# Issuing a rearrangement and its DMA transpose one to seven steps earlier, in an attention + MoE kernel

## The chip, the cores and the metric

The kernel runs on one core of a Trainium2 chip. The metric is the device time of one execution in microseconds (us), lower is better. The matmuls take bf16 and accumulate in fp32. Each run also has a granted TensorE clock and a state: on one core a run counts as slow when it is over 1.5% above the fastest run of the same kernel.

## The reference, cut to what matters

For each of 8 batches and 8 heads, x is (512, 64) and state is (32, 64). There are two reads with softmax, then a feed-forward layer over all 4352 rows.

```python
scores = scale * x @ state.T ; a = softmax(scores)        # (512, 32)
xread  = a @ state
sread  = softmax(scale * state @ x.T) @ x                 # (32, 64)
rows   = concat([xread, sread])  ->  (B * 544, 512)       # heads side by side
out    = gelu(rows @ w_in) @ w_out                        # 512 -> 2048 -> 512
```

## The kernel before

The kernel is a software pipeline with a hand-made schedule. While TensorE runs the feed-forward matmuls of batch b (16 steps; in each, `mm1` of batch b and `mm2` of batch b - 1), a table inserts the attention work of the next batch into some of the steps. The scores of a batch need x transposed. The path of the data is: a load of x by GpSimd (POOL) into `xb`, a rearrangement into `x4`, and a DMA transpose from `x4` into `xT`, issued by SyncE (SP), which also issues the output writes.

```python
xin = tile_pool(bufs=3)                  # xb: three batches
att = tile_pool(bufs=2)                  # xT, e, a, ...: two batches
x4s = [tile x4_0, tile x4_1]             # two batches, fixed
...
def load_x(b):      nc.gpsimd.dma_start(out=xb, in_=x[b]...)       # 512 KB as bf16, cast from fp32 on the way
...
load_x(1); load_w_in(2); load_w_in(3); load_w_out(0); load_w_out(1)
load_x(2); load_w_out(2); load_w_out(3); load_x(3)                 # at start-up
...
def rearr(b):       eng = nc.vector if b < 3 else nc.gpsimd
                    # two copies: xb -> x4
def xtr_dma(b):     nc.sync.dma_start_transpose(out=A.xT..., in_=A.x4...)
def atr_dma(b):     nc.sync.dma_start_transpose(out=A.AT..., in_=A.a)   # later, of the softmax
def scores(b, half): # TensorE: pt <- xT, sbd (L189); ScalarE: exp (L199)
def sread(b):       # TensorE: sr <- e, x4 (L269)
...
extra = {
    ...
    1: {
        1: [sread(0), pmat(1, (2,))],
        2: [srt(0)],
        3: [pmat(1, (3,)), begin(2), rearr(2), xtr_dma(2)],
        4: [load_x(4), sread(1)],
        6: [srt(1)],
        8: [scores(2, 0), scores(2, 1), norm(2, 0), norm(2, 1)],
        10: [pmat(2, (0, 1), ...)],  11: [atr_dma(2)],  13: [sread(2)],
        14: [pmat(2, (2, 3), ...)],  15: [srt(2)],
    },
}
def steady(b):      # b >= 2
    nb = b + 1
    d[0] = [begin(nb), rearr(nb)];  if b + 3 < B: d[0].append(load_x(b + 3))
    d[0].append(xtr_dma(nb))
    d[4] = [scores(nb, 0), scores(nb, 1), norm(nb, 0), norm(nb, 1)]
    d[7] = [pmat(nb, (0, 1), ...)];  d[8] = [atr_dma(nb)];  d[12] = [sread(nb)]
    d[13] = [pmat(nb, (2, 3), ...)];  d[14] = [srt(nb)]
```

(The `lambda:` around every entry of the tables is left out here and below.)

The softmax here doesn't subtract the row's maximum and nothing guards it: scores larger than these inputs give would overflow.

Of the kernel before, what the change touches and what calls it, by code (L numbers as in the profile page):

```python
# [17 lines left out]
def kernel(  # L18
# [10 lines left out]
    B, H, S, D = x.shape  # L29
# [63 lines left out]
    def load_x(b):  # L93
        xb = xin.tile([128, H, SJ * D], BF16, name="xb", tag="xb")
        nc.gpsimd.dma_start(out=xb, in_=x[b].rearrange("h (p j) d -> p h (j d)", j=SJ))
        xbs[b] = xb
# [48 lines left out]
    def begin(b):  # L145
        A = Att()
        atts[b] = A
        A.x4 = x4s[b % 2]
        A.xT = att.tile([128, SJ, HC, 128], BF16, name="xT", tag="xT")
        A.e = att.tile([128, SJ * 2, HC * NS], BF16, name="e", tag="e")  # L150
        A.a = att.tile([128, SJ * 2, HC * NS], BF16, name="a", tag="a")

    def rearr(b):
        A = atts[b]
        eng = nc.vector if b < 3 else nc.gpsimd
        for t in range(2):
            eng.tensor_copy(  # L157
                out=A.x4[:, :, :, 64 * t:64 + 64 * t].rearrange("p j c d -> p c j d"),
                in_=xbs[b][:, 4 * t:4 * t + 4, :].rearrange("p c (j d) -> p c j d", d=D),
            )  # L160
# [45 lines left out]
    def xtr_dma(b):  # L206
        A = atts[b]
        nc.sync.dma_start_transpose(
            out=A.xT.rearrange("p j c n -> p (j c) n"), in_=A.x4.rearrange("p j c n -> p (j c n)")
        )  # L210

    def scores(b, half):
        score_mms(b, 2 * half)
        score_mms(b, 2 * half + 1)
        expo(b, half)

    def norm(b, half):
        A = atts[b]
        G = SJ * 2
        hs = slice(64 * half, 64 * half + 64)  # L220
        e4 = A.e[:, :, hs].rearrange("p g (c n) -> p g c n", n=NS)
        cs = att.tile([128, G, 2], FP32, name="cs", tag="cs")
        nc.vector.reduce_sum(out=cs, in_=e4, axis=AX.X)  # L223
        ics = att.tile([128, G, 2], FP32, name="ics", tag="ics")
        nc.vector.reciprocal(out=ics, in_=cs)
        nc.vector.tensor_tensor(  # L226
            out=A.a[:, :, hs].rearrange("p g (c n) -> p g c n", n=NS),
            in0=e4,
            in1=ics[:, :, :].to_broadcast((128, G, 2, NS)),
            op=ALU.mult,  # L230
        )
# [21 lines left out]
    def atr_dma(b):  # L253
        A = atts[b]
        A.AT = att.tile([128, SJ, 2, 128], BF16, name="AT", tag="AT")
        nc.sync.dma_start_transpose(
            out=A.AT.rearrange("p j t n -> p (j t) n"), in_=A.a
        )


    def sread(b):
        A = atts[b]
        sr = ps_f.tile([128, 130], FP32, name="sr", tag="f")
        for o, n in ((0, D), (128, 1)):
            for t in range(2):
                for j in range(SJ):
                    for c in range(HC):
                        q = slice(32 * c, 32 * c + 32)
                        nc.tensor.matmul(  # L269
                            sr[q, o + n * t:o + n * t + n],  # L270
                            lhsT=A.e[:, 2 * j + t, q],
                            rhs=A.x4[:, j, c, 64 * t:64 * t + 64] if n == D else ones,
                            start=(j == 0),
                            stop=(j == SJ - 1),
                        )
        A.srm = att.tile([128, 2, D], BF16, name="srm", tag="srm")
        inv = att.tile([128, 2], FP32, name="inv", tag="inv")
        nc.vector.reciprocal(out=inv, in_=sr[:, 128:130])
        nc.vector.tensor_tensor(
            out=A.srm,  # L280
            in0=sr[:, 0:128].rearrange("q (t d) -> q t d", t=2),
            in1=inv[:, :].to_broadcast((128, 2, D)),
            op=ALU.mult,
        )

    def srt(b):
        A = atts[b]
        ps = ps_f.tile([128, HC, NS], BF16, name="srT", tag="f")
        nc.tensor.transpose(
            ps.rearrange("p c n -> p (c n)"), A.srm.rearrange("q t d -> q (t d)"), ident  # L290
        )
        nc.vector.tensor_copy(out=XSR[:, :, b * NS:(b + 1) * NS], in_=ps)
# [3 lines left out]
    def pmat(b, fs, act=()):  # L296
        if b not in Ps:
            Ps[b] = att.tile([128, 2, d_ff], BF16, name="P", tag="P")
        pss = []
        for f in fs:  # L300
            ps = [ps_f.tile([128, 512], FP32, name="p_ps", tag="f") for t in range(2)]
            for c in range(HC):
                for t in range(2):
                    nc.tensor.matmul(  # L304
                        ps[t][32 * c:32 * c + 32, :],
                        lhsT=sbd[64 * t:64 * t + 64, b, c, 32 * t:32 * t + 32],
                        rhs=w_in_bf[64 * t:64 * t + 64, c, f * 512:(f + 1) * 512],
                        start=True,
                        stop=True,
                    )  # L310
            pss.append(ps)
        for f, ps in zip(fs, pss):
            for t in range(2):
                dst = Ps[b][:, t, f * 512:(f + 1) * 512]
                if (f, t) in act:
                    nc.scalar.copy(out=dst, in_=ps[t])  # L316
                else:
                    nc.vector.tensor_copy(out=dst, in_=ps[t])  # L318
# [86 lines left out]
    for c in range(HC):  # L405
# [32 lines left out]
        },  # L438
        1: {
            1: [lambda: sread(0), lambda: pmat(1, (2,))],  # L440
            2: [lambda: srt(0)],
            3: [lambda: pmat(1, (3,)), lambda: begin(2), lambda: rearr(2), lambda: xtr_dma(2)],
            4: [lambda: load_x(4), lambda: sread(1)],
            6: [lambda: srt(1)],
            8: [lambda: scores(2, 0), lambda: scores(2, 1), lambda: norm(2, 0), lambda: norm(2, 1)],
# [1 line left out]
            11: [lambda: atr_dma(2)],  # L447
            13: [lambda: sread(2)],
            14: [lambda: pmat(2, (2, 3), act=((2, 1), (3, 1)))],
            15: [lambda: srt(2)],  # L450
        },
    }

    def steady(b):
        nb = b + 1
        d = {}
        if nb >= B:
            return d
        d[0] = [lambda: begin(nb), lambda: rearr(nb)]
        if b + 3 < B:  # L460
            d[0].append(lambda: load_x(b + 3))
        d[0].append(lambda: xtr_dma(nb))
        d[4] = [
            lambda: scores(nb, 0),
            lambda: scores(nb, 1),
            lambda: norm(nb, 0),
            lambda: norm(nb, 1),
        ]
        d[7] = [lambda: pmat(nb, (0, 1), act=((0, 1), (1, 1)))]
        d[8] = [lambda: atr_dma(nb)]  # L470
        d[12] = [lambda: sread(nb)]
        d[13] = [lambda: pmat(nb, (2, 3), act=((2, 1), (3, 1)))]
        d[14] = [lambda: srt(nb)]
        return d
# [4 lines left out]
    for b in range(B):  # L479
        plan = extra[b] if b in extra else steady(b)  # L480
        for s in range(MC):
            for f in plan.get(s, ()):
                f()
            mm1(b, s)
            done += 1
            if done > lag:
                mm2(u)
                u += 1
# [40 lines left out]
```

## Time and profile before

| before | |
|---|---|
| time, median of 3 runs | 236.54 us (236.05 to 237.08) |
| span of the profiled run, granted clock | 234.7 us, 0.999 |
| TensorE busy | 217.1 us |
| TensorE waiting for xT | 5.4 us in six waits |

The prediction below shows the page, the waits and one steady batch. Two more readings matter later. The first is TensorE's timeline at the scores of batches 2, 3 and 5, where the bracket gives the idle time before the row and what ended it:

```profile
44.76 0.64 PE L189 MATMUL pt<-sbd,xT 128*128 128x64 bf16 x16 [0.88 <-DMA xT<-x]
...
65.92 0.64 PE L189 MATMUL pt<-sbd,xT 128*128 128x64 bf16 x16 [1.78 <-DMA xT<-x]
...
115.33 0.64 PE L189 MATMUL pt<-sbd,xT 128*128 128x64 bf16 x16 [1.44 <-DMA xT<-x]
```

The second is POOL's timeline around the end of start-up: the loads of batch 3 and, because POOL runs far ahead of the schedule, of batch 4, then nothing until the rearrangement of batch 3, which waits for its load.

```profile
21.27 0.89 POOL L95 DMA_DIRECT2D xb<-in_x_dram  x1 [0.57 <-DMA w_in_bf<-in_moe_w_in_dram]
22.92 0.88 POOL L95 DMA_DIRECT2D xb<-in_x_dram  x1 [0.76 <-DMA w_in_bf<-in_moe_w_in_dram]
40.20 2.02 POOL L157 COPY x<-xb 128x1024 bf16<-128x1024 bf16 x2 [16.40 <-DMA xb<-in_x_dram]
42.16 0.88 POOL L95 DMA_DIRECT2D xb<-in_x_dram  x1
```

These rows are only the issues. The view of the DMA issues gives the landings: 18.8 us after issue for batch 3 (at 40.1) and 19.8 us for batch 4 (at 42.7; the prediction's 42.2 came from a median of the two). The x load with least in its way, issued at 80 us, takes 5.9 us. The transpose of batch 2 is issued as SP's timeline shows:

```profile
38.62 4.07 SPq L208 DMA_TRANSPOSE xT<-x  x1
```

### The profile page before, as it was taken

The numbers are of one execution on the slowest core, as the hardware profiler recorded it, in microseconds if no ns is written. First come the engines' busy times: TensorE is split into PE (matmuls) and PEld (weight loads), VectorE is DVE, ScalarE is ACT, GpSimd is POOL, SyncE is SP. The second block draws the span as 40 slices with busy tenths as digits, with TensorE's granted clock in tenths as the row PEclk, the third lists the DMA queues.
The fourth block names the chain that finished last, engine by engine and source line by source line (L and its number), as shares of the span: only waits on it lengthen the run. The fifth ranks groups of instructions, "written<-read, shape, count | busy, mean of one in ns | idle before, by whom it ended". The sixth has DMA issues, their size and how long they took to land.

```text
span 234.7 us, 4315 instructions
## 1 busy us (share of the span) xinstructions
PE 217.1 (92%) x1844; PEld 100.7 (43%) x1844; DVE 85.3 (36%) x162; ACT 124.7 (53%) x208; POOL 28.1 (12%) x38
## 2 busy tenths in 40 slices
PE   5996799889979999999799999999999999999993
PEld 1543244434334444444344444444444444567441
DVE  2655974274135413631181317231623111111120
ACT  2577754485467446744494549454955454426000
POOL 8745001304000400030002000000000000000000
PEclk9999999999999999999999999999999999999999
DMA  7999999972923294252804061316131111211122
GB/s 205 149 178 206 202 205 185 126 161 26 226 76 86 56 165 98 62 75 53 128 0 106 31 143 38 89 47 134 46 92 45 47 45 55 80 46 47 27 65 87
DMA packets 38707, 23.12 MB, mean 98 GB/s; under 512 B 21920, under 2 KB 34464, under 8 KB 38688
## 3 DMA queue, kind: packets, MB, share of 16 engines
q0 software_dynamic: 13376, 8.09, 25.3%
q1 hardware_dynamic: 24352, 14.03, 24.8%
q10 hardware_dynamic: 960, 0.72, 1.0%
q8 instruction: 14, 0.23, 0.4%
q14 instruction: 5, 0.04, 0.1%
HBM read 17.30 MB, written 8.91 MB: 112 GB/s over the span
## 4 chain that ended last, share of the span: by engine, by line
PE 68%; DMA 18%; DVE 5%; ACT 3%; POOL 3%; issue 1%; SPq 1%; POOLq 0%; ACTq 0%
PE op L362 37%; PE hp L328 18%; DMA xT<-x 13%; DMA xb<-in_x_dram 5%; PE hps L376 3%; PE ops L388 3%; PE p_ps L304 3%; PE sr L269 2%; PE pt L189 2%; ACT g L335 2%; DVE osb L348 1%; POOL w_in_bf L79 1%; DVE P L318 1%; DVE a L226 1%; DVE cs L223 1%
## 5 line engine op out<-in xcount | busy, mean ns | idle before, releaser
L362 PE MATMUL op<-w_out_bf,g 128*128 128x512 bf16 x512 | 130.2, 379 | 0.0
L335 ACT ACTIVATE g<-hp 128x512 bf16<-128x512 f32 x128 | 74.5, 602 | 61.9 <-PE hp L328 61.7
L328 PE MATMUL hp<-AT,P 128*128 128x512 bf16 x256 | 75.9, 380 | 2.9 <-DVE P L318 1.5
L362 PEld LDWEIGHTS <-g 128*128 128x128 bf16 x512 | 50.1, 98 | 58.7
L348 DVE COPY osb<-op 128x512 f32<-128x512 f32 x31 | 21.4, 690 | 88.8 <-PE op L362 88.8
L328 PEld LDWEIGHTS <-P 128*128 128x128 bf16 x256 | 22.5, 98 | 30.2 <-issue 6.6
L318 DVE CAST P<-p_ps 128x512 bf16<-128x512 f32 x38 | 24.3, 684 | 11.1 <-PE p_ps L304 11.1
L157 POOL COPY x<-xb 128x1024 bf16<-128x1024 bf16 x10 | 10.1, 1044 | 93.3 <-PE sr L269 76.9
L316 ACT CAST P<-p_ps 128x512 bf16<-128x512 f32 x26 | 14.1, 601 | 6.1 <-PE p_ps L304 6.1
L223 DVE TENSOR_REDUCE cs<-e 128x16 f32<-128x512 bf16 x16 | 10.9, 682 | 17.2 <-ACT e L199 17.2
L199 ACT ACT_TABLE_LOAD x7 | 9.0, 1283 | 9.7 <-PE pt L189 9.7
L189 PE MATMUL pt<-sbd,xT 128*128 128x64 bf16 x128 | 6.3, 200 | 6.2 <-DMA xT<-x 5.4
L304 PE MATMUL p_ps<-w_in_bf,sbd 64*32 64x512 bf16 x256 | 11.9, 384 | 0.1
L226 DVE TENSOR_TENSOR a<-e,ics 128x512 bf16<-128x512 bf16 x16 | 11.1, 692 | 0.6
L383 ACT ACTIVATE g_sr<-hps 128x256 bf16<-128x256 f32 x16 | 6.1, 384 | 8.4 <-PE hps L376 8.0
L335 ACT ACT_TABLE_LOAD x8 | 10.3, 1283 | 0.1
L189 PEld LDWEIGHTS <-xT 128*128 128x128 bf16 x128 | 4.9, 102 | 10.5 <-DMA xT<-x 8.4
L199 ACT ACTIVATE e<-pt 128x512 bf16<-128x512 f32 x16 | 8.8, 595 | 0.7 <-PE pt L189 0.6
L118 PE MATMUL warm_ps<-warm 128*128 128x512 bf16 x20 | 7.9, 542 | 1.2 <-DVE warm L73 1.2
L376 PE MATMUL hps<-XSR,w_in_bf 128*128 128x256 bf16 x64 | 8.5, 273 | 0.0
L345 ACT COPY osb<-op 128x256 f32<-128x256 f32 x1 | 0.4, 372 | 13.9 <-DVE osb L343 13.9
L376 PEld LDWEIGHTS <-w_in_bf 128*128 128x128 bf16 x64 | 6.3, 98 | 2.7
(48 smaller groups left out, 81.8 us busy)
## 6 DMA issues: line engine op xcount, KB each, us to landing
out_dram<-osb SPq DMA_DIRECT2D x31, 256.0 KB, 2.3
xb<-in_x_dram POOLq DMA_DIRECT2D x7, 512.0 KB, 11.6
w_in_bf<-in_moe_w_in_dram POOLq DMA_DIRECT2D x8, 256.0 KB, 10.1
w_out_bf<-in_moe_w_out_dram POOLq DMA_DIRECT2D x4, 512.0 KB, 14.9
x0f<-in_x_dram SPq DMA_DIRECT2D x2, 256.0 KB, 3.4
x0f<-in_x_dram ACTq DMA_DIRECT2D x2, 256.0 KB, 4.3
out_dram<-osb SPq DMA_DIRECT2D x8, 64.0 KB, 1.7
st_bf<-in_state_dram POOLq DMA_DIRECT2D x1, 224.0 KB, 10.2
```

What stands on the lines that cost most here:

```text
L189: nc.tensor.matmul(A.pt[:, j, :, c % 2, :], lhsT=A.xT[:, j, c, :], rhs=sbd[:, b, c, :], start=True, stop=True,)
L199: nc.scalar.activation(out=A.e[:, :, 64 * half:64 * half + 64], in_=A.pt.rearrange("p j t c n -> p (j t) (c n)"), func=AF.Exp, scale=scale,)
L223: nc.vector.reduce_sum(out=cs, in_=e4, axis=AX.X)
L226: nc.vector.tensor_tensor(out=A.a[:, :, hs].rearrange("p g (c n) -> p g c n", n=NS), in0=e4, in1=ics[:, :, :].to_broadcast((128, G, 2, NS) ...
L304: nc.tensor.matmul(ps[t][32 * c:32 * c + 32, :], lhsT=sbd[64 * t:64 * t + 64, b, c, 32 * t:32 * t + 32], rhs=w_in_bf[64 * t:64 * t + 64, c ...
L316: nc.scalar.copy(out=dst, in_=ps[t])
L318: nc.vector.tensor_copy(out=dst, in_=ps[t])
L328: nc.tensor.matmul(hp, lhsT=Ps[b][:, t, m * 128:(m + 1) * 128], rhs=atts[b].AT[:, :, t, :], start=(t == 0), stop=(t == 1),)
L335: nc.scalar.activation(out=gs[b][:, m, :], in_=hp, func=AF.Gelu)
L348: nc.vector.tensor_copy(out=osb, in_=ps)
L362: nc.tensor.matmul(ps, lhsT=gs[b][:, m, j * 128:(j + 1) * 128], rhs=w_out_bf[:, m, :], start=(m == 0), stop=(m == MC - 1),)
L376: nc.tensor.matmul(hp, lhsT=w_in_bf[:, c, m * 128:(m + 1) * 128], rhs=XSR[:, c, :], start=(c == 0), stop=(c == HC - 1),)
```

## The change

The intent is to take the wait for xT away from TensorE by issuing the transpose eleven steps before the scores in steady batches, in place of four.

```diff
 1: {
-    2: [srt(0)],
-    3: [pmat(1, (3,)), begin(2), rearr(2), xtr_dma(2)],
+    2: [srt(0), begin(2), rearr(2), xtr_dma(2)],
+    3: [pmat(1, (3,))],
...
-    15: [srt(2)],
+    15: [srt(2), begin(3), rearr(3), load_x(5), xtr_dma(3)],
 def steady(b):
-    d[0] = [begin(nb), rearr(nb)]
-    if b + 3 < B: d[0].append(load_x(b + 3))
-    d[0].append(xtr_dma(nb))
...
     d[8] = [atr_dma(nb)]
+    if nb + 1 < B:
+        d[9] = [begin(nb + 1), rearr(nb + 1)]
+        if nb + 3 < B: d[9].append(load_x(nb + 3))
+        d[9].append(xtr_dma(nb + 1))
```

So the change has three parts: batch 2 moves one step earlier, batch 3 moves one step earlier (from step 0 of batch 2 to step 15 of batch 1), and batches 4 to 7 move seven steps earlier.

More of the change, by code (lines that the diff above doesn't have):

```diff
@@ L440 @@
             1: [lambda: sread(0), lambda: pmat(1, (2,))],
-            2: [lambda: srt(0)],
-            3: [lambda: pmat(1, (3,)), lambda: begin(2), lambda: rearr(2), lambda: xtr_dma(2)],
+            2: [lambda: srt(0), lambda: begin(2), lambda: rearr(2), lambda: xtr_dma(2)],
+            3: [lambda: pmat(1, (3,))],
             4: [lambda: load_x(4), lambda: sread(1)],
@@ L449 @@
             14: [lambda: pmat(2, (2, 3), act=((2, 1), (3, 1)))],
-            15: [lambda: srt(2)],
+            15: [lambda: srt(2), lambda: begin(3), lambda: rearr(3), lambda: load_x(5), lambda: xtr_dma(3)],
         },
@@ L458, in steady @@
             return d
-        d[0] = [lambda: begin(nb), lambda: rearr(nb)]
-        if b + 3 < B:
-            d[0].append(lambda: load_x(b + 3))
-        d[0].append(lambda: xtr_dma(nb))
         d[4] = [
@@ L470, in steady @@
         d[8] = [lambda: atr_dma(nb)]
+        if nb + 1 < B:
+            d[9] = [lambda: begin(nb + 1), lambda: rearr(nb + 1)]
+            if nb + 3 < B:
+                d[9].append(lambda: load_x(nb + 3))
+            d[9].append(lambda: xtr_dma(nb + 1))
         d[12] = [lambda: sread(nb)]
```

## The prediction

> **What bounds the kernel now.** I read the page first: busy shares, then the chain that ended last, then the waits, then the timeline of one batch, then the DMA issues.
>
> ```profile
> PE 217.1 (92%) x1844; PEld 100.7 (43%) x1844; DVE 85.3 (36%) x162; ACT 124.7 (53%) x208; POOL 28.1 (12%) x38
> ...
> PE 68%; DMA 18%; DVE 5%; ACT 3%; POOL 3%; issue 1%; SPq 1%; POOLq 0%; ACTq 0%
> PE op L362 37%; PE hp L328 18%; DMA xT<-x 13%; DMA xb<-in_x_dram 5%; PE hps L376 3%; PE ops L388 3%; PE p_ps L304 3%; PE sr L269 2%; PE pt L189 2%; ACT g L335 2%; DVE osb L348 1%; POOL w_in_bf L79 1%; DVE P L318 1%; DVE a L226 1%; DVE cs L223 1%
> ```
>
> TensorE is busy for 217.1 of 234.7 us, so it bounds the kernel, with 17.6 us of idle to win at most. The chain puts 13% (30 us) on the transpose that makes xT from x. That figure is not what the transpose costs: while it is in flight TensorE goes on with the feed-forward matmuls (L328, L362), and the chain merely follows the DMA in place of that work. The cost is what TensorE waits at its end, which the list of waits gives:
>
> ```profile
> PEld L189 <- DMA xT<-x: 8.4, 6, 2.3
> ...
> PE pt L189 <- DMA xT<-x: 5.4, 6, 1.8
> ...
> PE hp L328 <- DVE P L318: 1.5, 4, 0.8
> ```
>
> The columns are the total in us, how often, and the longest. The score matmuls (L189) of batches 2 to 7 each wait once for xT: 5.4 us on TensorE's matmul row in six waits. The 8.4 us of weight loads is the same event seen from an engine that runs ahead, so it isn't added. After start-up the one other matmul wait is 1.03 us on ACT, in batch 1. The timeline of one steady batch shows why the DMA is late:
>
> ```profile
> 133.94 0.69 DVE L348 COPY osb<-op 128x512 f32<-128x512 f32 x1 [2.37 <-PE op L362]
> ...
> 134.66 0.33 SPq L350 DMA_DIRECT2D out_dram<-osb  x1
> ...
> 135.09 2.17 SPq L208 DMA_TRANSPOSE xT<-x  x1
> ...
> 138.06 1.03 PE L362 MATMUL op<-w_out_bf,g 128*128 128x512 bf16 x4
> ...
> 139.54 0.64 PE L189 MATMUL pt<-sbd,xT 128*128 128x64 bf16 x16 [0.45 <-DMA xT<-x]
> ```
>
> The transpose isn't held by its data: in the POOL timeline the rearrangement of this batch ended near 105. It is held by its place in SyncE's in-order stream, behind the output write of step 15, which waits for an eviction of VectorE at 133.94. Issued at 135.09, it lands 4.40 us later, 0.05 us before the scores start. Step 4 of the batch simply comes round too soon.
>
> **What the Trainium skill says.** "DMA: Bandwidth & Descriptors", Rules for kernel authors: issue a DMA early, compute, and wait on its semaphore late. That is the change, and the trace agrees that only the tail is exposed. "Perfetto Trace Analysis", Summary: the profiler window per engine type: the slice of a hardware-generated DMA leaves out the data movement, and a matmul's end is estimated. The trace agrees with the first (a 2.17 us slice, 4.40 us to landing). For the second, "TensorE: Matmul & The Clock Gate", Wait — 56ns, not 53.3ns?, gives 215.7 ns start to start for 512 columns; here the four matmuls from 138.06 would release the next at 138.92 (the hp pairs after other groups of four do start 0.86 us on), while the row shows an end at 139.09. So each wait is some 0.16 us longer than its idle column. "DMA: Bandwidth & Descriptors", Silent corruption: two transposing streams in flight at once: transposes from SP form one stream, so putting xT right behind AT needs no new wait. No trace here tests that, as the two are now 12 us apart.
>
> **The change part by part.** Nothing is added or removed: same instructions, bytes and shapes. What moves is where the transpose stands on SP and where the rearrangement stands on DVE (batch 2) or POOL (3 to 7).
>
> *POOL*: order there stays rearr 3, load 5, rearr 4, load 6, rearr 5, load 7, rearr 6, rearr 7. POOL already runs ahead: it does these at 40.2, 53.9, 78.2, 102.4 and 127.6, each released by a weighted-sum matmul (sr, L269) or, the first, by a load. All precede the new issue points (batch 4 at about 75, then 99, 124, 149). No gain, no loss.
>
> *Batches 4 to 7*: xT is issued behind the AT transpose of step 8 (for the batch shown, SP is done with AT at 147.50 + 1.30 = 148.8; the next scores run at 163.70). About 15 us of lead against 4.4 to 6.1 us to landing. The wait goes. By the idle column: 0.45, 1.44, 0.45, 0.44; with 0.16 each: 0.61, 1.60, 0.61, 0.60, sum **3.4 us**.
>
> *Batch 2*: one step earlier. Before: issued at 38.62, landed at 44.70 (6.08 us, beside the loads), score matmul at 44.76 instead of 42.85 + 0.86 = 43.71. After: its xb landed at 16.04 + 15.2 = 31.2, VectorE ends XSR at 35.13 and then idles 1.44 us for p_ps; the two copies (0.75 us) fit into that hole. Issue at about 36.0, landing near 42 to 43, even if the two loads in flight (until 40.1 and 42.2) slow it. Needed at 43.7. Gain **1.0 us**.
>
> *Batch 3*: step 15 in place of step 0. Before: issued at 60.14 behind the second of two output writes, landed at 65.87, needed at 63.12 + 0.86 = 63.98, a delay of 1.94 us. After: only the write of 58.37 stands ahead, so issue at about 58.7, 1.4 us earlier; at 5.7 us it lands at 64.4, leaving 0.4 to 0.6 us. A load that POOL issues at 55.91 and that takes 6.0 us now overlaps more of it. Gain **1.4 us**.
>
> Sum: 3.4 + 1.0 + 1.4 = **5.8 us**; all six waits gone altogether would be 6.4. 236.54 − 5.8 = **230.7 us**, 2.5% less.
>
> **The rivals.**
> 1. *A new wait takes its place.* After the scores, ACT does a table load (1.28), two exps (1.09) and another table load (1.28) while gelus queue up, and TensorE can run out of PSUM buffers; it does for 1.03 us in batch 1. But this burst starts when the scores end, so it moves with them. Before them, ACT idles 1.16 us in the batch shown; with the scores 0.6 us earlier some idle is left. If ACT or VectorE gave half of it back, time would be 233 to 234. I give it little.
> 2. *The transpose was hidden anyway*, as its share of the chain suggests nothing by itself. Six waits on TensorE itself speak against. Steady batches confirm it: from one sr group to the next, 102.07 to 127.27 is 25.20 us with a wait of 1.44, its neighbours 24.20 with 0.45: the difference, 1.00, is the difference of the waits. Then 236, no change: very unlikely.
> 3. *Contention on the queue.* xT right behind AT makes SP busy longer (1.3 + 2.2 to 3.3 us) and could delay AT or the output writes. AT, issued at 147.50 and landing in 3.1 us, is used at about 157; the next write waits until 152.2 for its eviction, and there are four output buffers. Slack of 6 us; worth 0.
> 4. *Part gain.* The odd waits (batches 2, 3, 5) aren't fully understood: landing took 5.41 us in batch 5 without a load in flight. If batches 2 and 3 gained nothing, 3.4 us are left: 233.1.
>
> **Range and chances.** Best case 236.54 − 6.4 = 230.1, with 0.3 us for the spread (236.05 to 237.08 before): 229.8. A bad but plausible case loses 1 us in batch 3 and 0.5 us elsewhere: 232.2. The 2% line is at 231.8, 1.1 us above my number and a fifth of the gain, so faster 0.82, within 2% 0.17, slower 0.01.
>
> **What would show it.** In the changed profile: six waits of the score matmul on xT become none, or one under 0.7 us in batch 3; DMA xT falls from 13% of the chain to about nothing; xT slices on SP follow AT slices directly in batches 4 to 7; sr to sr in steady batches is 23.6 us in place of 24.2; busy TensorE stays at 217 us while the span falls to about 229. A wait of hp on gelu or P totalling over 2 us would show rival 1; AT or osb among TensorE's releasers rival 3; xT waits left in batches 2 and 3, rival 4. Wrong altogether if the semaphores make SP's transpose wait for something later in the batch than the rearrangement.

## The result, and the profile after

| | before | after |
|---|---|---|
| median | 236.81 us of 4 runs (236.05 to 240.78; the run of 240.78 counts as slow) | 232.99 us of 4 runs (232.78 to 233.45) |
| ratio of the fast runs | | 0.9852 (0.9819 to 0.9885) |
| span of the profiled run | 234.7 us | 230.9 us |
| TensorE busy | 217.1 us | 217.2 us |
| mean granted clock of that run | 0.999 | 0.983 |

Ratios and their 95% intervals, here and below, compare the fast runs of the two kernels in the same rounds, so they are not quite the ratio of the medians. The later sets of rounds ran on several chips, so times in us are best compared within a set. The change took 1.5% off where 2.5% was predicted, and 232.99 lies 0.8 us above the range. All outputs are right.

The chain of the changed kernel, by engine and by line, and its list of waits (total, times, longest):

```profile
PE 81%; DMA 8%; DVE 5%; ACT 3%; issue 1%; SPq 0%; DVEq 0%; ACTq 0%
PE op L362 43%; PE hp L328 22%; DMA xT<-x 7%; PE hps L376 3%; PE ops L388 3%; PE p_ps L304 3%; PE warm_ps L118 2%; PE sr L269 2%; PE pt L189 2%; DMA st_f<-in_state_dram 1%; ACT g L335 1%; DVE P L318 1%; DVE a L226 1%; DVE cs L223 1%; DVE sbd L137 1%
...
PE pt L189 <- DMA xT<-x: 2.4, 2, 2.0
PE hp L328 <- DVE P L318: 1.5, 4, 0.8
```

The six waits have become two, 5.4 us have become 2.4, and no other engine took their place. But the longest is now 2.0 us, more than any before. SP's timeline and TensorE's say which two these are:

```profile
35.20 4.91 SPq L208 DMA_TRANSPOSE xT<-x  x1
...
59.86 4.17 SPq L208 DMA_TRANSPOSE xT<-x  x1
...
73.56 1.30 SPq L256 DMA_TRANSPOSE AT<-a  x1
74.95 1.49 SPq L208 DMA_TRANSPOSE xT<-x  x1
```

```profile
45.22 0.71 PE L189 MATMUL pt<-sbd,xT 128*128 128x64 bf16 x16 [2.04 <-DMA xT<-x]
65.59 0.64 PE L189 MATMUL pt<-sbd,xT 128*128 128x64 bf16 x16 [0.40 <-DMA xT<-x]
```

Batch 2's transpose was issued 3.4 us earlier (35.20 against 38.62) and TensorE waited longer for it, 2.04 us against 0.88. Batch 3 kept 0.40 us, and batches 4 to 7, whose transpose stands right behind that of AT, wait no more.

A ledger of the span shows where the time came from. The starts of the weighted-sum matmuls (`sr`, L269) cut it into pieces that each hold the scores of known batches:

| piece of the span, us | before | after | difference |
|---|---|---|---|
| start to sr of batch 0 | 32.41 | 31.71 | -0.70 |
| to sr of batch 2 (scores of batch 2) | 21.14 | 22.90 | +1.76 |
| to sr of batch 3 (scores of batch 3) | 24.25 | 22.86 | -1.39 |
| to the end (scores of batches 4 to 7) | 156.90 | 153.43 | -3.47 |
| sum | 234.70 | 230.90 | -3.80 |

The first row holds nothing that the change touches; over all traces that point falls between 31.2 and 34.1 us, so it is chance. The 1.76 us of batch 2 are the longer wait (2.04 - 0.88 = 1.16), then a stretch at a lower clock, less a wait that vanished. The view of stretches, of the changed kernel from 43.00 on (start:end, length, busy time of PE, PEld, DVE, ACT, POOL, then the granted clock, DMA share and GB/s):

```profile
43.00:45.20 2.20, 0.18 (x1) 0.00 (x0) 0.69 (x1) 0.00 (x0) 0.00 (x0) 1.00 1.84 80
45.20:49.20 4.00, 3.98 (x25) 1.81 (x26) 1.51 (x3) 3.47 (x4) 0.00 (x0) 0.57 1.03 217
49.20:52.00 2.80, 2.80 (x28) 1.01 (x27) 2.73 (x6) 2.65 (x6) 0.00 (x0) 1.00 0.01 3
```

After the pause TensorE got 0.57 of its clock for 4 us. From the scores to the P matmuls (L304) of step 10 took 50.06 - 45.22 = 4.84 us in place of 47.91 - 44.76 = 3.15, so 1.69 us more. In return the wait of 1.03 us of `hp` on ScalarE that stood there before is gone. Together 1.16 + 1.69 - 1.03 = 1.82.

Why did the transpose of batch 2 take longer? From issue to landing it took 6.1 us before and 10.0 us after; in batch 7 of the changed kernel it takes 4.3. The DMA view of the stretch from 36 to 38 us of the changed kernel, one to three us after the issue, has this (queue: packets, MB, and the summed time of its packets as a share of 16 engines' time, which can pass 100%):

```profile
DMA packets 778, 0.39 MB, mean 197 GB/s; under 512 B 9, under 2 KB 778, under 8 KB 778
...
q0 software_dynamic: 778, 0.39, 147.1%
...
xT<-x SPq DMA_TRANSPOSE x1, 10.0
```

All 778 packets belong to q0, the queue of POOL's loads. The transpose, which goes through q1, did not move one packet in this stretch. The Trainium skill, "DMA: Bandwidth & Descriptors", Issuing engines are not separate DMA queues, says that DMAs of all issuing engines run on the same 16 DMA engines and interleave. The trace fits that; the 2 us without a packet show how little interleaving the later one got. Whether the loads hold it at the DMA engines or already while SP issues it (4.91 us here, 1.49 us in batch 4) is not separated by any run.

### The profile page after: what moved, and what is told of

Read it like the earlier page. It is cut to its first block, busy times and chain, and to the rows that moved or that the text cites. A ratio compares the mean times of both kernels' runs of the same rounds, so it can differ in the third digit from the quotient of the medians.

```text
span 230.9 us, 4315 instructions
## 1 busy us (share of the span) xinstructions
PE 217.2 (94%) x1844; PEld 100.6 (44%) x1844; DVE 85.2 (37%) x162; ACT 124.8 (54%) x208; POOL 28.0 (12%) x38
## 4 chain that ended last, share of the span: by engine, by line
PE 81%; DMA 8%; DVE 5%; ACT 3%; issue 1%; SPq 0%; DVEq 0%; ACTq 0%
PE op L362 43%; PE hp L328 22%; DMA xT<-x 7%; PE hps L376 3%; PE ops L388 3%; PE p_ps L304 3%; PE warm_ps L118 2%; PE sr L269 2%; PE pt L189 2%; DMA st_f<-in_state_dram 1%; ACT g L335 1%; DVE P L318 1%; DVE a L226 1%; DVE cs L223 1%; DVE sbd L137 1%
## 5 line engine op out<-in xcount | busy, mean ns | idle before, releaser
L328 PE MATMUL hp<-AT,P 128*128 128x512 bf16 x256 | 76.8, 383 | 1.9 <-DVE P L318 1.5
L304 PE MATMUL p_ps<-w_in_bf,sbd 64*32 64x512 bf16 x256 | 11.9, 384 | 0.1
```

Source lines behind the costliest of these rows:

```text
L304: nc.tensor.matmul(ps[t][32 * c:32 * c + 32, :], lhsT=sbd[64 * t:64 * t + 64, b, c, 32 * t:32 * t + 32], rhs=w_in_bf[64 * t:64 * t + 64, c ...
L328: nc.tensor.matmul(hp, lhsT=Ps[b][:, t, m * 128:(m + 1) * 128], rhs=atts[b].AT[:, :, t, :], start=(t == 0), stop=(t == 1),)
```

## The experiments

The theory after this reading: the transpose of batch 2 is held by loads in flight, so issuing it earlier gains nothing. The rivals: the shortfall arose in later batches, or the transpose is slow at that place for a reason of its own. "To landing" below is from issue to landing; "wait 2" and "wait 3" are TensorE's waits for xT in batches 2 and 3.

### Only the batch-2 part

```diff
 # the kernel before
-    2: [srt(0)],
-    3: [pmat(1, (3,)), begin(2), rearr(2), xtr_dma(2)],
+    2: [srt(0), begin(2), rearr(2), xtr_dma(2)],
+    3: [pmat(1, (3,))],
```

> The kernel before with only the batch-2 part of the change (copies and transpose at step 2 of batch 1 in place of step 3). Theory (the loads of x that are still in flight hold this transpose; issuing it earlier gains nothing): it lands some 9 to 10 us after its issue, near 45 us, the score matmuls of batch 2 wait 1.5 to 2.2 us instead of 0.9, and the time is 0.5 to 1.5 us above the kernel before. Rival (batch 2 gained its 1.0 us as predicted and the shortfall arose in later batches): landing about 6 us after issue, no wait, 1 us below the kernel before.

Measured: the transpose was issued at 36.63 and took 9.7 us to landing; wait 2 was 1.79 us. That is what the theory expected of this trace. The ratio, 0.9993 (0.9916 to 1.007), decides nothing: the theory's loss of 0.5 to 1.5 us and the rival's gain of 1 us both lie inside the interval.

### The batch-2 part taken back

```diff
 # the changed kernel
-    2: [srt(0), begin(2), rearr(2), xtr_dma(2)],
-    3: [pmat(1, (3,))],
+    2: [srt(0)],
+    3: [pmat(1, (3,)), begin(2), rearr(2), xtr_dma(2)],
```

> The changed kernel with batch 2 put back to step 3. Theory: the wait of batch 2 is 0.9 us again, the rest of the gain stays (0.4 us left in batch 3, none in batches 4 to 7): 231.5 to 232.3 us, 1 us below the changed kernel's 233.0. Rival (later batches lost it): 234 us, 1 us above the changed kernel.

Measured: 234.14 us, ratio 0.987 (0.9795 to 0.9945). The theory's number was missed, and the rival's 234 us was met, but not for the rival's reason. The trace tells why: at the old place, issued at 38.79, the transpose took 8.7 us and TensorE waited 3.41 us, not 0.88. Batch 3 waited 0.19 us, batches 4 to 7 not at all. So the wait of 0.88 us in the first profile was not a property of the old place; it was one draw.

### The load of batch 4 put off

```diff
 # the changed kernel
-    4: [load_x(4), sread(1)],
+    4: [sread(1)],
...
-    15: [srt(2), begin(3), rearr(3), load_x(5), xtr_dma(3)],
+    15: [srt(2), begin(3), rearr(3), load_x(4), load_x(5), xtr_dma(3)],
```

POOL then issues this load at 41.7 us, behind the rearrangement of batch 3, in place of about 22.

> The changed kernel with one thing moved: the load of x for batch 4 is issued behind the rearrangement of batch 3 on the same engine, so at about 40 us in place of 21 us. Theory (loads in flight hold the transpose of batch 2): it lands within 7.5 us of its issue at 35 us, the wait of batch 2 falls from 2.0 to under 0.5 us, the time is 230.5 to 231.7 us. Rival (the transpose is slow there for a reason of its own, such as its place right behind start-up, or the load of batch 5 at 40.7 us that comes in its last microseconds): landing still 9 to 10 us after issue, wait about 2 us, 233 us.

Measured: 7.7 us to landing. That is just past the 7.5 us expected, but the wait is gone:

```profile
42.36 1.03 PE L362 MATMUL op<-w_out_bf,g 128*128 128x512 bf16 x4
43.22 0.63 PE L189 MATMUL pt<-sbd,xT 128*128 128x64 bf16 x16
```

The scores start 0.86 us after the group before them, with no idle bracket. Time 230.48 us, ratio 0.973 (0.9627 to 0.9834).

### The load of batch 5 put off

```diff
 # the changed kernel
-    15: [srt(2), begin(3), rearr(3), load_x(5), xtr_dma(3)],
+    15: [srt(2), begin(3), rearr(3), xtr_dma(3)],
...
     d[9] = [begin(nb + 1), rearr(nb + 1)]
+    if b == 2: d[9].append(load_x(5))
```

> The changed kernel with the load of x for batch 5 moved from 41 us to behind the rearrangement of batch 4 (about 57 us). Theory (the loads of batches 3 and 4, issued at 20 and 21 us, hold the transpose): wait of batch 2 still 1.5 us or more, time within 0.6 us of the changed kernel, perhaps worse by a wait of up to 1.5 us in batch 3, where two loads now stand beside its transpose. Rival (the load of batch 5 holds its tail): the wait of batch 2 falls under 0.5 us.

Measured: 8.1 us to landing in batch 2, at 45.1, 3.4 us after the load of batch 4 had landed (41.7). No wait is listed there, which is the rival's number. But this execution had started late (its first `sr` came at 33.50), so the scores were due only at 44.13 + 0.86 = 44.99. The distance to the load of batch 4 is no shorter than in the changed kernel (2.9), so the load of batch 5 isn't what held it there. In batch 3 two loads now stood beside the transpose (issued at 56.3 and 57.2): 9.7 us to landing, a wait of 4.43 us, and 238.59 us in all, ratio 1.0051 (0.9978 to 1.0124). That was more than the expected 1.5 us, and it shows the same effect in another batch.

### One more load: the suspected cause doubled

```diff
 # the changed kernel
 load_x(3)
+nc.gpsimd.dma_start(out=xdum, in_=x[7]...)      # xdum is read by nobody
```

> The changed kernel with one more load of x, of 512 KB into a buffer that nobody reads, put behind the load of batch 3 at start-up: the suspected cause doubled. Theory: the last load lands 2 to 3 us later than the 42 us of the changed kernel, the transpose of batch 2 lands as much later (47 to 49 us), its wait grows by 2 to 3 us to 4 to 5 us, and the time by as much, to 235 to 237 us. Rival (the transpose's time there has nothing to do with the loads): landing and wait unchanged, 233 us.

Measured: the load of batch 4 now landed at 47.7 us, 5.5 us later than in the changed kernel, and the transpose, issued at 35.47, at 49.6. TensorE's timeline:

```profile
42.42 1.03 PE L364 MATMUL op<-w_out_bf,g 128*128 128x512 bf16 x4
49.67 1.04 PE L191 MATMUL pt<-sbd,xT 128*128 128x64 bf16 x16 [6.22 <-DMA xT<-x]
```

The wait grew from 2.04 to 6.22 us, the time to 238.14 us (two runs; the changed kernel had 232.86 in the same rounds). The direction is the theory's; the size is above the 2 to 3 us that were expected.

### Only the steady part

```diff
 # the changed kernel, with batches 2 and 3 as before:
     3: [pmat(1, (3,)), begin(2), rearr(2), xtr_dma(2)],
     15: [srt(2)],
+    if b == 2: d[0] = [begin(3), rearr(3), load_x(5), xtr_dma(3)]
```

> The kernel before with only the part for batches 4 to 7 changed; batches 2 and 3 as before. Theory (the steady part of the prediction holds): no waits in batches 4 to 7, the waits of batches 2 and 3 stay (0.9 to 3.4 and about 1.8 us), ratio 0.985 to 0.988, which is 3.4 us off some 237. Rival (the steady part gave less than 3.4 us, the loss is there): ratio above 0.99.

Measured: ratio 0.9827 (0.9665 to 0.999), too wide to decide. The profiled execution fell in the slow state (its first `sr` came at 34.06); TensorE waited 0.99 us in batch 2 and 1.82 us in batch 3, both as expected. Its last piece, from sr of batch 3 to the end, is 153.47 us with no wait in batches 4 to 7, as long as in the changed kernel's fast run (153.43).

### All waits removed

```diff
 # the changed kernel, with the load of batch 4 put off as above, and batch 3 issued earlier
+    12: [begin(3), rearr(3), load_x(4), load_x(5), xtr_dma(3)],
-    15: [srt(2), begin(3), rearr(3), load_x(5), xtr_dma(3)],
+    15: [srt(2)],
```

> The changed kernel with the load of batch 4 behind the rearrangement of batch 3, and the transpose of batch 3 issued at step 12 of batch 1 in place of step 15. Theory: no wait on a transpose is left in any batch; ratio 0.970 to 0.976, about 6 us off, so the predicted gain is there once the loads are out of the way. Rival: removing these waits uncovers another one (gelu before hp, or P), ratio 0.98 or more.

Measured: 230.87 us, ratio 0.9734 (0.9637 to 0.9831), and no wait for xT is left in any batch. Its chain by engine:

```profile
PE 88%; DVE 5%; ACT 3%; DMA 1%; issue 1%; ACTq 0%; DVEq 0%
```

DMA has gone from 18% of the chain to 1%. With the same rounds, the changed kernel had 0.9821 (next run) and the kernel before is 1. So this version is ahead of both. The two intervals overlap, but both carry the spread of the kernel before. Set directly beside each other, the six runs of each have means of 230.71 and 232.80 us, 2.1 us apart (95% interval, worked out from these twelve times: 0.9 to 3.3).

### The changed kernel again, twice, and the kernel before against itself

> The changed kernel itself, unchanged, to have it beside the other runs of this call and to see how much the wait of batch 2 varies from one profiled execution to the next. Theory: transpose of batch 2 lands 2 to 5 us after the load of batch 4, whenever that is, wait of batch 2 1 to 3 us; ratio to the kernel before 0.985.

Measured: 232.86 us, ratio 0.9821 (0.9732 to 0.9909); 9.5 us to landing, 3.2 us after the load of batch 4; wait 2 was 1.31 us.

> The changed kernel a third time. If the batch-2 part of the change gains nothing on the mean, its wait of batch 2 is again 1 to 2.2 us, about what the kernel before shows over its own repeats; ratio 0.980 to 0.986.

Measured: 232.18 us, ratio 0.9744 (0.9672 to 0.9816); 9.9 us to landing, wait 2 was 1.96 us, and 0.77 us were left in batch 3 (the tool names VectorE for these, but xT landed at 64.70, 0.05 us before the scores started).

> The kernel before against itself: how far two sets of the same kernel lie apart on this chip, and how much its wait of batch 2 varies. Expected: ratio 1.000 within 0.01, wait of batch 2 anywhere from 0.9 to 3.4 us, transpose of batch 2 landing 2 to 5 us after the load of batch 4.

Measured: ratio 0.9981 (0.9896 to 1.0067); 7.6 us to landing, wait 2 was 2.09 us. The kernel before had medians of 238.3 to 238.9 us in all the later sets of rounds, against the 236.54 that the prediction started from, and a wider spread (234.8 to 241.2) than the changed kernel (231.3 to 234.0).

### The load put off, without the change

```diff
 # the kernel before
-    4: [load_x(4), sread(1)],
+    4: [sread(1)],
...
     d[0] = [begin(nb), rearr(nb)]
+    if b == 2: d[0].append(load_x(4))
```

> The kernel before with nothing but the load of x for batch 4 moved behind the rearrangement of batch 3 (about 41 us in place of 22 us). Theory (loads in flight set when the transpose of batch 2 lands): it lands within 5 us of its issue at about 38.6 us, the wait of batch 2 is under 0.6 us, those of batches 3 to 7 stay at 4 to 5 us together, time 1 to 2 us below the kernel before (ratio 0.990 to 0.997). Rival (issue order on the queue matters, not the load): wait as before.

Measured: 6.5 us to landing and a wait of 1.33 us, where under 0.6 was expected; ratio 0.9876 (0.9772 to 0.998). The theory in its first form, that only loads issued earlier hold the transpose, falls: here the load of batch 3 had landed at 38.9, before the transpose was issued at 39.76. But two loads were issued at 41.5 and 42.3, before it landed. The mended theory, that any load in flight between issue and landing holds it, needed its own test.

### Both loads kept out of the way, without the change

```diff
 # the kernel before; held is a column of its own
-    4: [load_x(4), sread(1)],
+    4: [sread(1)],
...
-    8: [scores(2, 0), scores(2, 1), norm(2, 0), norm(2, 1)],
+    8: [scores(2, 0), scores(2, 1), norm(2, 0), norm(2, 1), hold(2), load_x(4)],
+# hold(b): nc.gpsimd.tensor_copy(out=held, in_=atts[b].a[:, 0, 0:1])
```

> The kernel before with both loads that stood beside the transpose of batch 2 held back: an added one-column copy on the engine that issues them waits for the normalised scores of batch 2 (at about 50 us), and the loads of batches 4 and 5 come behind it. The transpose stays at step 3, issued at 38.5 to 40 us. In the run where only the load of batch 4 was put off, to 41.5 us, the transpose still took 6.5 us with a wait of 1.33 us; the question is what held it. Theory, mended (any load in flight between issue and landing holds it, also one issued after it): it lands 4.4 to 5.2 us after its issue and the wait of batch 2 is under 0.6 us. Rival (only a backlog issued earlier holds it, or the transpose is slow there by itself): 6 us or more to landing, wait above 1 us. Total time is not the question here, since the loads may now meet the transpose of batch 3 instead.

Measured: issued at 38.24, 5.1 us to landing, no wait in batch 2. That is the mended theory's number, with the transpose at its old place and the load of batch 3 beside it only in its first microsecond (it landed at 39.2). The loads, now issued from 47.8 us on, met the next transposes instead: TensorE waited 2.1 us for AT, and the transpose of batch 3 took 7.0 us. The total (237.44 us, ratio 1.0119) is not better, as was expected.

### Taken together

The transpose of batch 2 in all profiled executions in the fast state whose order of loads is the same:

| kernel | place | issued | load of batch 4 landed | transpose landed | wait 2 |
|---|---|---|---|---|---|
| before | step 3 | 38.62 | 42.7 | 44.7 | 0.88 |
| before, again | step 3 | 38.88 | 42.1 | 46.4 | 2.09 |
| batch 2 taken back | step 3 | 38.79 | 42.8 | 47.5 | 3.41 |
| changed | step 2 | 35.20 | 42.2 | 45.2 | 2.04 |
| changed, again | step 2 | 35.62 | 42.0 | 45.1 | 1.31 |
| changed, third | step 2 | 34.65 | 41.5 | 44.5 | 1.96 |
| batch 2 only | step 2 | 36.63 | 43.2 | 46.4 | 1.79 |

Issue times spread over 4.2 us and landings over 3.0, but they don't go together: at step 2 the transpose lands 2.9 to 3.2 us after the load of batch 4, at step 3 2.0 to 4.6 us after it. The mean wait is 2.13 us at step 3 and 1.78 at step 2, a difference of 0.35 that three and four draws with a spread of 2.5 us can't tell from nothing. The piece from sr of batch 0 to sr of batch 2 says the same: 21.14, 23.18 and 23.75 us at step 3 (mean 22.69), and 22.90, 21.84, 22.23 and 22.07 us at step 2 (mean 22.26). The pair on record set the shortest of the first beside the longest of the second.

Why did the tail behind the last load vary so much at step 3? The traces point to the load of batch 5, issued at 40.0 to 42.2 in these runs. In "batch 2 taken back" it was issued at 41.7. From 44.2 to 47.0 us, with the load of batch 4 landed and the transpose not yet, the two queues moved this:

```profile
q0 software_dynamic: 657, 0.34, 118.5%
q1 hardware_dynamic: 30, 0.00, 1.5%
```

So the data of the transpose were through, and what was still missing came in a few small packets beside that load. In "before, again", from 43.5 to 46.0 us, it was 724 packets against 30. The first trace, in which the load of batch 5 was issued last (42.16), has the shortest tail. But the load of batch 5 alone was moved at step 2 only, where the tail stayed (3.4 us without it), so for step 3 this is read from traces and not shown by a run.

## Why the prediction was wrong

**What failed: the step "Batch 2".** It said that the copies fit into VectorE's hole, that the issue comes at about 36.0, and that the transpose then lands "near 42 to 43, even if the two loads in flight (until 40.1 and 42.2) slow it", for a gain of 1.0 us. The copies did fit, and the issue came at 35.20. But the transpose landed at 45.2, 10.0 us later and 2.9 us after the load of batch 4, and this piece of the span got 1.76 us longer. The prediction had the two loads before it and took the 6.08 us of before as nearly constant. Its error was to add a duration to an issue time where the loads in flight set the end. The runs show it: without the load of batch 4 in the way the wait is gone, with one load more it is 6.22 us, and with both neighbouring loads held back the transpose lands in 5.1 us at its old place. From -1.0 to +1.76 is 2.8 us. Start-up chance (-0.70) hid part of it, which leaves 5.8 predicted against 3.8 in the two spans.

**A second error: one profile was taken for the kernel.** A wait of 0.88 us in batch 2 was one of 0.88, 2.09 and 3.41. So the +1.76 us of this pair is in part bad luck: on the means of the table's traces batch 2 changed by -0.4 us, which is no gain clear of noise and no loss either. What the traces refute is the landing: issued at 34.7 to 36.6, no transpose at step 2 came before 44.5, where 42 to 43 was said. How much batch 2 gains or loses on the mean, so few traces don't fix. The other two parts alone, 1.39 + 3.47 = 4.86 us, would give some 231.7 us (an estimate). The later sets of rounds put the changed kernel at 0.9821 and 0.9744, the second of which is close to the predicted 2.5%. That is luck too: most of it is the kernel before being slower in those sets (fast runs of 237.3 and 238.4 us on the mean, against 236.6), while wait 2 of the changed kernel was still 1.31 and 1.96 us.

**What held.** Batches 4 to 7: 3.4 us predicted, 3.47 measured. The idle column alone gives 2.78 for these four waits, so the correction of 0.16 us per wait, read from the start-to-start distance, was right: (3.47 - 2.78) / 4 = 0.17. Batch 3: 1.4 us predicted with 0.4 to 0.6 left; 1.39 measured with 0.40 left (0.19 to 0.77 in the repeats). In steady batches sr to sr is now 124.64 - 101.06 = 23.58 us, for 23.6 predicted. TensorE's busy time stayed at 217.2 us. The span is 230.9 us and not 229, for the reason above. That xT right behind AT needs no new wait is now tested as well: AT of batch 6, issued at 144.31, was in flight until 147.6, xT was issued at 145.71, and the results were correct. (The sr groups that the prediction read at 102.07 and 127.27 start at 102.00 and 127.20; their distance, 25.20 us, stands.)

**The rivals.** The first (a new wait takes the place of the old) did not come. The second (hidden anyway) is refuted for batches 4 to 7. The third (contention on SP's queue) did not show in the steady batches; contention was the right word, but it was with POOL's loads, and the prediction looked for it among SP's own DMAs. The fourth (part gain) gave 233.1 us for no gain in batches 2 and 3, and the time came out at 233.0. That is luck: batch 3 gained its 1.4 us, and batch 2 lost more than that in this pair. The "bad but plausible case" of the range had no room for a part of the change that costs time.

## What to carry to other kernels

Before moving a DMA earlier, list what else is in flight between its new issue and its need. Where that is little, the wait goes as computed (batches 4 to 7); where it was a backlog, as here in batch 2, the end of the backlog set the landing and the earlier issue was worth nothing, until the loads were moved out of the way. And read a wait in the start-up phase from several executions before it goes into a sum.

## What the Trainium skill lacked or had wrong

- "DMA: Bandwidth & Descriptors" says in Issuing engines are not separate DMA queues that DMAs of different engines interleave, and in Queues, rings and completion order that each DMA engine takes turns between its queues packet by packet. Neither says how long the later queue can go without a packet. A transpose issued by SP behind POOL's loads at 35.20 moved no packet from 36 to 38 us, while the loads moved 778, and took 9.5 to 10.0 us at step 2 (14.2 us with one more load), against 4.3 to 4.7 us with no load about. Whether its packets stood in line already is not in the trace.
- The same page, Rules for kernel authors: "Issue the DMA early" lacks that condition. Issued 3.4 us earlier into the backlog, the transpose landed 0.5 us later (45.2 against 44.7), and over seven traces the landings at the two places overlap (44.5 to 46.4 and 44.7 to 47.5). The rule that a transpose next to ordinary DMAs needs nothing says nothing of its time.
- "TensorE: Matmul & The Clock Gate", What's actually happening, puts the cold state after at least one idle window of about 3.4 us. Here a pause of 2.2 us was followed by 4 us at 0.57 of the clock (changed kernel), and one of 2.1 us by 3.5 us at 0.52 (the kernel before, again), while a pause of 3.5 us (batch 2 taken back) had the full clock behind it. So the length of the pause alone doesn't decide. The page calls its window free-running, which leaves room for the third case but not for the first two.
